# Retention and MLP on one core: merged key and query transfers, W_in rows in head order through split weight transfers, and a rearranged start

## The chip, the core and the metric

The kernel runs on one core of a Trainium2 chip. The metric is device time in microseconds (us); with one core the slowest core is that core. "PE" is TensorE, "PEld" its weight loads, "DVE" VectorE, "ACT" ScalarE, "POOL" GpSimd, "SP" SyncE.

## The reference

Four sequences of 768 tokens with 8 heads of 64 go through a retention layer, and its output through an MLP with weights in float64.

```python
batch, n_heads, seq, head_dim = (4, 8, 768, 64)
n_tokens, d_model, d_ff = (3072, 512, 2048)

for t in range(S):                                     # retention
    state = gamma[None, :, None, None] * state + np.einsum('bhd,bhe->bhde', k[:, :, t], v[:, :, t])
    y[:, :, t] = scale * np.einsum('bhd,bhde->bhe', q[:, :, t], state)
# x = y as (B*S, H*D)
h = x @ w_in                                           # MLP
sp = np.maximum(h, 0.0) + np.log1p(np.exp(-np.abs(h)))
g = h * erf(sp)
return (g @ w_out).astype(np.float32)
```

Only the q, k, v inputs are cast to float32. W_in (512 x 2048) and W_out (2048 x 512) arrive as 8-byte words, and the kernel makes float32 of them on DVE and ACT.

## The kernel before

The tokens are cut into 24 chunks of 128. A chunk's keys, queries and values are 256 KB each, in rows of 64 floats, that is, in packets of 256 bytes. The weights come in 16 pieces of 1 MB, in rows of 256 words, that is, in packets of 2 KB. The chunks fill three rotating buffers; the weight pieces fill four raw areas, each reloaded as soon as its piece is converted.

DVE scales the keys and queries of a chunk, masks its scores, and converts weights between these in a fixed order. Keys and queries are loaded so that heads (0, 3), (1, 2), (4, 7), (5, 6) lie side by side, and that takes four transfers each:

```python
PAIRS = ((0, 3), (1, 2), (4, 7), (5, 6))
MOVES = ((0, 0), (3, 1), (1, 2), (2, 3))
def load(j):
    ...
    for i, src in enumerate((k, q)):
        queue = nc.scalar if i and j < 3 else nc.sync
        for of, to in MOVES:
            queue.dma_start(
                KQ[j][:, i].rearrange("p (a b) d -> p a b d", a=2)[:, :, to],
                src[b, :, now, :].rearrange("(a b) p d -> p a b d", a=2)[:, :, of],
            )
    nc.sync.dma_start(V[j], v[b, :, now, :].rearrange("h p d -> p h d"))

def load_piece(n):                       # a W_in piece: one transfer into all 128 partitions
    ...
    nc.sync.dma_start(
        w.rearrange("p (g f) -> p g f", g=n_k),
        w_in[:, i * 2 * P : (i + 1) * 2 * P].rearrange("(g p) f -> p g f", p=P),
    )
```

The pairing lets the retention output land in PSUM in just the row order that W_in has, so two wide copies per chunk finish it:

```python
def place(h, r):
    return pp[r][h % 2 * D : (h % 2 + 1) * D, h // 4, :]
...
for r in range(2):
    nc.scalar.copy(XC[m][:, r::2, i * C : (i + 1) * C], pp[r][:, :2, :])
```

The start:

```python
nc.scalar.dma_start(d_k, decay_k)
load(0)
for s in range(2):
    nc.scalar.dma_start(d_s[:, s], ...)       # a small transfer, 2 KB each
load(1)
load_piece(0)
load(2)
load_piece(1)
ident = const.tile([P, P], F32, name="ident")
make_identity(nc, ident)
... # 28 dummy transposes on PE
```

Of the kernel before, what the change touches and what calls it, by code (L numbers as in the profile page):

```python
# [12 lines left out]
F32 = mybir.dt.float32  # L13
# [6 lines left out]
P = 128  # L20
# [6 lines left out]



PAIRS = ((0, 3), (1, 2), (4, 7), (5, 6))  # L30
MOVES = ((0, 0), (3, 1), (1, 2), (2, 3))


IN = {"11": 0, "12": 1, "21": 2, "22": 3, "S3": 2, "S1": 4, "S2": 5, "S4": 6}
# [12 lines left out]
def kernel(  # L47
# [13 lines left out]
    nc = tc.nc  # L61
    B, H, S, D = q.shape
# [4 lines left out]
    n_k = d_model // P  # L67
# [4 lines left out]
    DH = d_model // 2  # L72
# [3 lines left out]
    const = ctx.enter_context(tc.tile_pool(name="const", bufs=1))  # L76
# [9 lines left out]
    KQ, V = {}, {}  # L86

    def load(j):
        b, c = divmod(j, NC)
        KQ[j] = loads.tile([P, 2, H, D], F32, name="kq")  # L90
        V[j] = loads.tile([P, H, D], F32, name="v")
        now = slice(c * C, (c + 1) * C)
        for i, src in enumerate((k, q)):

            queue = nc.scalar if i and j < 3 else nc.sync
            for of, to in MOVES:
                queue.dma_start(  # L97
                    KQ[j][:, i].rearrange("p (a b) d -> p a b d", a=2)[:, :, to],
                    src[b, :, now, :].rearrange("(a b) p d -> p a b d", a=2)[:, :, of],
                )  # L100
        nc.sync.dma_start(V[j], v[b, :, now, :].rearrange("h p d -> p h d"))

    kq_s = const.tile([P, NC, 2, H], F32, name="kq_s")
    d_k = const.tile([P, H], F32, name="d_k")
    d_s = const.tile([P, 2, HP], F32, name="d_s")

    w_in_sb = const.tile([P, 2, 7, 2, FG * P], F32, name="w_in_sb")
    w_out_sb = const.tile([P, 2, 7, FG, DH], F32, name="w_out_sb")
# [26 lines left out]
    place = [n % 4 if n < n_p - 4 else (n - n_p + 4) % 3 for n in range(n_p)]  # L135

    def load_piece(n):
        which, i = pieces[n]
        w = raws[place[n]]
        if which == "in":  # L140
            nc.sync.dma_start(
                w.rearrange("p (g f) -> p g f", g=n_k),
                w_in[:, i * 2 * P : (i + 1) * 2 * P].rearrange("(g p) f -> p g f", p=P),
            )
        else:
            for d in range(2):
                nc.sync.dma_start(
                    w.rearrange("p (d f c) -> p d f c", d=2, f=2)[:, d],
                    w_out[i * 2 * P : (i + 1) * 2 * P, d * DH : (d + 1) * DH].rearrange(
                        "(f p) c -> p f c", p=P  # L150
                    ),
                )

    def load_pieces_after(n):
        for later in range(n + 1, n_p):
            if place[later] == place[n]:
                load_piece(later)
                break
# [95 lines left out]
    def pace(n):  # L254

        nonlocal room
        room += n
        while room >= 1:
            next(weight_steps, None)
            room -= 1  # L260

    def need(*what):
        nonlocal room
        while what not in done:
            if next(weight_steps, done) is done:
                next(last_steps)
            room -= 1

    nc.scalar.dma_start(d_k, decay_k)
    load(0)  # L270
    for s in range(2):
        nc.scalar.dma_start(d_s[:, s], decay_s[s * D : s * D + 1, :].to_broadcast([P, HP]))
    load(1)
    load_piece(0)
    load(2)
    load_piece(1)

    ident = const.tile([P, P], F32, name="ident")
    make_identity(nc, ident)

    causal = const.tile([P, C], F32, name="causal")
    nc.gpsimd.memset(causal, 1.0)
# [4 lines left out]
    state = const.tile([P, HP, D], F32, name="state")  # L287
# [4 lines left out]
    def query_scale(c):  # L292
        nc.vector.reciprocal(kq_s[:, c, 1], kq_s[:, c, 0])
        nc.vector.tensor_scalar(kq_s[:, c, 1], kq_s[:, c, 1], unscale, None, op0=ALU.mult)

    def in_pairs(to, of):
        for a, b in MOVES:
            nc.vector.tensor_copy(
                to.rearrange("p (a b) -> p a b", a=2)[:, :, b],
                of.rearrange("p (a b) -> p a b", a=2)[:, :, a],  # L300
            )

    in_pairs(kq_s[:, 0, 0], d_k)
    query_scale(0)

    def other_scales():
        back, by = (const.tile([P, H], F32, name=name) for name in ("back", "by"))
        nc.vector.reciprocal(back, d_s.rearrange("p s h -> p h s"))
        in_pairs(by, back)
        for c in range(1, NC):  # L310
            nc.gpsimd.tensor_tensor(kq_s[:, c, 0], kq_s[:, c - 1, 0], by, op=ALU.mult)
        query_scale(slice(1, NC))


    QT, KT, SC, AM, XC, SU = {}, {}, {}, {}, {}, {}
# [3 lines left out]


    idle = ps_o.tile([P, P], F32, name="o0")
    for _ in range(28):
        nc.tensor.transpose(idle, ident, ident)

    def ret_psum():

        pool = next(psum_turn) if early else ps_r
        return pool.tile([P, HP, C], F32, name="hp" if pool is ps_h else "r")
# [49 lines left out]
    def ret_out(j):  # L378
        c = j % NC
        m, i = divmod(j, JPC)  # L380
        if i == 0:
            XC[m] = ret.tile([P, HP, TCH], F32, name="xT")

        pp = [ret_psum() for _ in range(2)]

        def place(h, r):
            return pp[r][h % 2 * D : (h % 2 + 1) * D, h // 4, :]



        if c:
            for u, pair in enumerate(PAIRS):
                for r, h in enumerate(pair):
                    own = slice(r * D, (r + 1) * D)
                    nc.tensor.matmul(  # L395
                        place(h, r), state[own, u, :], QT[j][own, u, :],
                        start=(h < 4), stop=False, skip_group_check=True,
                    )
        for h in range(H):
            u, r = next((u, pair.index(h)) for u, pair in enumerate(PAIRS) if h in pair)  # L400
            nc.tensor.matmul(  # L401
                place(h, r), V[j][:, h, :], AM[j][:, r, u, :],
                start=(not c and h < 4), stop=True, skip_group_check=True,
            )
        for r in range(2):
            nc.scalar.copy(XC[m][:, r::2, i * C : (i + 1) * C], pp[r][:, :2, :])  # L406
        pace(1.5)

    def ret_state(j):
        c = j % NC  # L410
        if c < NC - 1:
            p = SU[j] = ret_psum()
            for u, pair in enumerate(PAIRS):
                for r, h in enumerate(pair):
                    nc.tensor.matmul(  # L415
                        p[r * D : (r + 1) * D, u, :D], KQ[j][:, 0, 2 * u + r, :], V[j][:, h, :],
                        start=True, stop=True,
                    )
            pace(1)
        if j + 3 < NJ:  # L420
            load(j + 3)
        if j < 2:
            load_piece(j + 2)
# [89 lines left out]
    def chunk_of(g):  # L513
        return TCH // SCH + (g - G0) // 2
# [104 lines left out]
    def put_part(m, step):  # L619
# [26 lines left out]

    K_, T, S_, M, O_, U, A = (
        ret_scale, ret_transpose, ret_scores, ret_mask, ret_out, ret_state, ret_add
    )


    K_(0)
    other_scales()
    T(0)
    n_first = 6
# [40 lines left out]
    j = 2 * JPC  # L696
# [50 lines left out]
    g, m = NG - 1, chunk_of(NG - 1)  # L747
# [47 lines left out]
```

## Time and profile before

| What | Value |
|---|---|
| Time | 754.32 us median of 6 (753.08 to 755.75) |
| Span of the profiled execution | 751.6 us |
| Scaling of chunk 5 | 45.13 us, after a wait of 3.33 us |
| Dense PE stretch begins | 82.93 us |
| 2 KB packets, mean of the whole execution | 93.5 ns |
| 256-byte packets, mean of the whole execution | 18.2 ns |

The groups of transfers of before (what is written <- what is read, engine, count, KB each, median us from issue to landing):

```profile
kq<-in_k_dram SPq DMA_DIRECT2D x96, 64.0 KB, 2.6
...
w_in_sb<-in_moe_w_in_dram SPq DMA_DIRECT2D x6, 1024.0 KB, 5.6
...
w_out_sb<-in_moe_w_in_dram SPq DMA_DIRECT2D x2, 1024.0 KB, 6.8
```

The raw words of W_in land in spare parts of either weight tile, hence two rows for it: 6 + 2 transfers of a whole megabyte, and 96 small ones for the keys. The order of time on SP's queue shows the issues for chunk 5 (start, duration, line, what it fills, count):

```profile
35.34 2.00 SPq L97 DMA_DIRECT2D kq<-in_k_dram  x4
37.39 5.09 SPq L97 DMA_DIRECT2D kq<-in_q_dram  x4
42.52 1.47 SPq L101 DMA_DIRECT2D v<-in_v_dram  x1
```

Nine issues from 35.34 to 43.99 us; the last queries are issued shortly before 42.5 us and the scaling that needs them starts at 45.13.

### The profile page before, as it was taken

The page shows a single profiled execution, that of the slowest core. Times are in us where ns is not written, and L with a number is a line of the kernel's source. Part 1 is how long each engine was busy: PE and PEld are TensorE (multiplying, and loading weights), DVE is VectorE, ACT ScalarE, POOL GpSimd, SP SyncE. Part 2 cuts the span into 40 slices and gives each one's busy share as a digit, 9 for nine tenths or more (in the row PEclk, how much of TensorE's full clock was granted, in tenths as well). Part 3 has the DMA queues.
Part 4 walks back from the last instruction along what each step waited for, and adds up shares of the span by engine and source line. Part 5 has one row for each costly group of instructions (what it writes and reads, how often), then busy time and mean ns, then how long its engine had stood idle before and what let it go on. Part 6 is the DMA issues. An engine that isn't in the chain of part 4 may idle for free.

```text
span 751.6 us, 12027 instructions
## 1 busy us (share of the span) xinstructions
PE 724.5 (96%) x5244; PEld 609.3 (81%) x5244; DVE 353.4 (47%) x470; ACT 274.1 (36%) x319; POOL 32.4 (4%) x28
## 2 busy tenths in 40 slices
PE   6877999999999999999999999999999999999997
PEld 5644444457789999999999999999999999999995
DVE  3878899975554424333243153153163152153323
ACT  1323555341532433424414424424334244324440
POOL 1000200000010110110110110101100000000000
PEclk8999999999999999999999999999999999999999
DMA  8885634101110120120120120110100000000000
GB/s 192 238 227 171 195 117 164 56 0 43 57 43 19 25 71 9 36 72 1 43 72 1 43 71 1 43 51 22 43 29 1 2 29 1 1 29 1 1 29 28
DMA packets 89700, 42.73 MB, mean 57 GB/s; under 512 B 78384, under 2 KB 78384, under 8 KB 89648
## 3 DMA queue, kind: packets, MB, share of 16 engines
q1 hardware_dynamic: 85952, 41.17, 19.7%
q10 hardware_dynamic: 3696, 0.80, 0.5%
q8 instruction: 41, 0.67, 0.4%
q14 instruction: 11, 0.09, 0.0%
HBM read 35.66 MB, written 6.29 MB: 56 GB/s over the span
## 4 chain that ended last, share of the span: by engine, by line
PE 88%; DVE 4%; DMA 4%; ACT 1%; SPq 1%; issue 1%; ACTq 0%; DVEq 0%
PE hp L544 34%; PE o L604 32%; PE o L487 7%; PE hp L474 6%; PE r L361 3%; PE r L401 2%; PE r L348 2%; DMA w_out_sb<-in_moe_w_out_dram 2%; PE r L415 1%; PE r L395 1%; DMA kq<-in_q_dram 1%; DVE am L373 1%; SPq L97 1%; DMA w_in_sb<-in_moe_w_in_dram 1%; DVE kq L339 0%
## 5 line engine op out<-in xcount | busy, mean ns | idle before, releaser
L544 PE MATMUL hp<-xs,w_in_sb 128*128 128x128 f32 x1280 | 158.7, 278 | 0.0
L544 PEld LDWEIGHTS hp<-xs,w_in_sb 128*128 128x128 f32 x1280 | 150.4, 192 | 6.6 <-issue 3.2
L604 PE MATMUL o<-w_out_sb,h 128*128 128x256 f32 x640 | 141.6, 379 | 0.0
L463 DVE TENSOR_TENSOR e<-h,e 128x1024 f32<-128x1024 f32 x44 | 53.6, 1260 | 178.5 <-ACT e L444 178.5
L604 PEld LDWEIGHTS o<-w_out_sb,h 128*128 128x128 f32 x640 | 121.7, 190 | 16.5
L544 PE MATMUL hp<-xT,w_in_sb 128*128 128x128 f32 x960 | 113.7, 275 | 0.0
L544 PEld LDWEIGHTS hp<-xT,w_in_sb 128*128 128x128 f32 x960 | 112.0, 192 | 1.9 <-issue 1.0
L604 PE MATMUL o<-w_out_sb,e 128*128 128x256 f32 x480 | 111.5, 382 | 0.9 <-DVE e L463 0.9
L604 PEld LDWEIGHTS o<-w_out_sb,e 128*128 128x128 f32 x480 | 88.2, 190 | 12.5 <-DVE e L463 1.3
L443 ACT ACT_TABLE_LOAD x24 | 30.8, 1283 | 91.2 <-PE o L604 89.1
L474 PE MATMUL hp<-xT,w_in_sb 128*128 128x512 f32 x128 | 57.6, 605 | 0.0
L572 DVE TENSOR_TENSOR h<-h,hp 128x512 f32<-128x512 f32 x20 | 13.8, 688 | 86.7 <-PE hp L544 86.7
L339 POOL TENSOR_TENSOR kq<-kq,kq_s 128x1024 f32<-128x1024 f32 x15 | 30.3, 2019 | 499.8 <-DMA kq<-in_q_dram 401.1
L474 PEld LDWEIGHTS hp<-xT,w_in_sb 128*128 128x128 f32 x128 | 24.5, 195 | 29.4 <-issue 28.7
L567 DVE TENSOR_TENSOR h<-h,hp 128x512 f32<-128x512 f32 x20 | 13.8, 688 | 71.1 <-ACT h L565 71.1
L443 ACT ACTIVATE e<-h 128x2048 f32<-128x2048 f32 x22 | 42.0, 1910 | 0.2
L444 ACT ACTIVATE e<-e 128x2048 f32<-128x2048 f32 x22 | 42.0, 1910 | 0.2
L406 ACT COPY xT<-r 128x256 f32<-128x256 f32 x42 | 13.9, 375 | 74.8 <-PE r L401 74.8
L570 ACT COPY h<-hp 128x512 f32<-128x512 f32 x20 | 11.7, 585 | 70.8 <-PE hp L544 70.8
L373 DVE TENSOR_TENSOR am<-r,causal 128x512 f32<-128x512 f32 x42 | 27.2, 683 | 20.3 <-PE r L361 15.9
L361 PE MATMUL r<-qT,kT 64*128 64x128 f32 x336 | 29.9, 291 | 4.6 <-ACT qT L354 4.5
L348 PE MATMUL r<-ident,kq 128*128 128x128 f32 x168 | 24.0, 285 | 9.3 <-DMA kq<-in_k_dram 4.9
(91 smaller groups left out, 667.6 us busy)
## 6 DMA issues: line engine op xcount, KB each, us to landing
w_out_sb<-in_moe_w_out_dram SPq DMA_DIRECT2D x14, 512.0 KB, 5.0
kq<-in_k_dram SPq DMA_DIRECT2D x96, 64.0 KB, 2.6
v<-in_v_dram SPq DMA_DIRECT2D x24, 256.0 KB, 3.6
w_in_sb<-in_moe_w_in_dram SPq DMA_DIRECT2D x6, 1024.0 KB, 5.6
out_dram<-r SPq DMA_DIRECT2D x24, 256.0 KB, 2.3
kq<-in_q_dram SPq DMA_DIRECT2D x84, 64.0 KB, 2.5
w_out_sb<-in_moe_w_in_dram SPq DMA_DIRECT2D x2, 1024.0 KB, 6.8
w_in_sb<-in_moe_w_out_dram SPq DMA_DIRECT2D x2, 512.0 KB, 4.9
```

The costliest lines, as they stand in the source:

```text
L339: engine.tensor_tensor(KQ[j], KQ[j], by, op=ALU.mult)
L348: nc.tensor.transpose(p[:, u, :], KQ[j][:, i, 2 * u : 2 * u + 2, :].rearrange("p h d -> p (h d)"), ident,)
L361: nc.tensor.matmul(pp[s][:, hp, :], KT[j][s * D : (s + 1) * D, hp, :], QT[j][s * D : (s + 1) * D, hp, :], start=True, stop=True,)
L373: nc.vector.tensor_tensor(AM[j][:, s], SC[j][s], causal[:, None, :].to_broadcast([P, HP, C]), op=ALU.mult)
L401: nc.tensor.matmul(place(h, r), V[j][:, h, :], AM[j][:, r, u, :], start=(not c and h < 4), stop=True, skip_group_check=True,)
L443: nc.scalar.activation(E[g], HS[g], AF.Softplus)
L444: nc.scalar.activation(E[g], E[g], AF.Erf)
L463: nc.vector.tensor_tensor(E[g][:, half], HS[g][:, half], E[g][:, half], op=ALU.mult)
L474: nc.tensor.matmul(p, w_in_of(ft, kk), XC[0][:, kk, :], start=(kk == 0), stop=(kk == n_k - 1))
L487: nc.tensor.matmul(O[0][tt].rearrange("p (d c) -> p d c", d=2), E[g][:, u * TCH + tt * P : u * TCH + (tt + 1) * P], w_out_of(ft), start=(f ...
L544: nc.tensor.matmul(bank[:, u, :], w_in_sb[:, s, IN[a], kk, u * P : (u + 1) * P], XS[m][b][:, kk, :], start=(p in (1, 2, 5) and u == 0 and ...
L604: nc.tensor.matmul(O[m][i][:, half, :], G[g][a][:, u * P : (u + 1) * P], w_out_sb[:, s, OUT[b], u, :], start=i not in started, stop=(s == ...
```

## The change

The intent: load keys and queries of a chunk in one transfer each, with the heads in their own order, and pay for that in the weights rather than at every chunk. With natural pairs (0, 1), (2, 3) and so on, the retention output comes out in another row order; W_in's rows are loaded in that order, which needs two transfers per piece, each into 64 partitions. Apart from that, the first weight pieces are sent right behind chunk 0, the identity is made first, ten dummy matmuls take the place of 28 transposes, and a tiny ACT copy draws the activation table in early.

```diff
-PAIRS = ((0, 3), (1, 2), (4, 7), (5, 6))
-MOVES = ((0, 0), (3, 1), (1, 2), (2, 3))
+PAIRS = (0, 2, 1, 3)
@@ load
-            for of, to in MOVES:
-                queue.dma_start(... [:, :, to], ... [:, :, of])
+            queue.dma_start(KQ[j][:, i], src[b, :, now, :].rearrange("h p d -> p h d"))
@@ load_piece
-            nc.sync.dma_start(
-                w.rearrange("p (g f) -> p g f", g=n_k),
-                w_in[:, i * 2 * P : (i + 1) * 2 * P].rearrange("(g p) f -> p g f", p=P),
-            )
+            for r in range(2):
+                nc.sync.dma_start(
+                    w[r * D : (r + 1) * D].rearrange("p (g f) -> p g f", g=n_k),
+                    w_in[r * DH : (r + 1) * DH, i * 2 * P : (i + 1) * 2 * P].rearrange(
+                        "(g p) f -> p g f", p=D
+                    ),
+                )
@@ start
+    ident = const.tile([P, P], F32, name="ident")
+    make_identity(nc, ident)
     nc.scalar.dma_start(d_k, decay_k)
     load(0)
+    nc.scalar.copy(idle_out, ident[:, :1])
     for s in range(2):
         nc.scalar.dma_start(d_s[:, s], ...)
+    load_piece(0)
     load(1)
-    load_piece(0)
+    load_piece(1)
     load(2)
-    load_piece(1)
-    ident = const.tile([P, P], F32, name="ident")
-    make_identity(nc, ident)
@@ dummies
-    for _ in range(28):
-        nc.tensor.transpose(idle, ident, ident)
+    for _ in range(10):
+        nc.tensor.matmul(idle, ident, ident, start=True, stop=True)
@@ ret_out
-            return pp[r][h % 2 * D : (h % 2 + 1) * D, h // 4, :]
+            return pp[h % 2][h // 4 * D : (h // 4 + 1) * D, h % 4 // 2, :]
... (the loops over heads follow the natural pairs; a few tiny copies of scales fall away)
```

## The prediction

> **What bounds the kernel now.** I read the engine shares first, then the activity by slices, then ten-microsecond windows, then the chain of waits, and last the order of time on VectorE (DVE) and on the queue of SyncE (SP). From the page:
>
> ```profile
> PE 724.5 (96%) x5244; PEld 609.3 (81%) x5244; DVE 353.4 (47%) x470; ACT 274.1 (36%) x319; POOL 32.4 (4%) x28
> ...
> PE   6877999999999999999999999999999999999997
> ...
> DVE  3878899975554424333243153153163152153323
> ```
>
> Read the slices, not the averages: PE is at 9 from the sixth slice on. Only the first four or five slices (18.8 us each) have room, so a change that leaves the later matmuls alone can only move the moment at which the dense stretch begins. The chain of waits names that moment:
>
> ```profile
> 82.93 13.93 PE hp L474 x32
> 96.86 13.73 PE o L487 x32
> ```
>
> From 82.9 us the chain is PE nearly all the way to 751.6. Before it, the windows (PE, PEld, DVE, ACT, POOL busy; granted clock; DMA share; GB/s):
>
> ```profile
> 0.00:10.00 10.00, 6.12 (x36) 5.64 (x36) 2.67 (x13) 0.00 (x0) 2.15 (x13) 1.00 0.64 137
> 10.00:20.00 10.00, 6.41 (x46) 5.16 (x48) 5.42 (x8) 3.94 (x7) 0.00 (x0) 0.59 1.03 270
> 20.00:30.00 10.00, 8.33 (x124) 6.48 (x120) 7.84 (x11) 3.09 (x6) 0.00 (x0) 0.89 0.64 183
> 30.00:40.00 10.00, 8.64 (x132) 6.87 (x136) 9.64 (x13) 4.61 (x9) 0.00 (x0) 1.00 1.02 308
> 40.00:50.00 10.00, 5.32 (x66) 4.18 (x61) 5.28 (x7) 1.82 (x4) 0.00 (x0) 0.83 0.70 163
> 50.00:60.00 10.00, 9.66 (x65) 5.40 (x64) 9.21 (x11) 4.34 (x7) 0.00 (x0) 1.00 0.89 234
> ```
>
> DVE, which scales keys and queries, masks scores and converts the weights in a fixed order, is nearly full from 22 us on, except at 40:50, where DMA was full just before. The order of time shows what DVE waited for; also why the start is late on ScalarE (ACT):
>
> ```profile
> 10.39 1.28 ACT L354 ACT_TABLE_LOAD   x1 [10.39 <-DMA kq<-in_k_dram]
> ...
> 14.92 0.69 DVE L373 TENSOR_TENSOR am<-r,causal 128x512 f32<-128x512 f32 x1 [4.42 <-PE hp L361]
> ...
> 45.13 1.23 DVE L339 TENSOR_TENSOR kq<-kq,kq_s 128x1024 f32<-128x1024 f32 x1 [3.33 <-DMA kq<-in_q_dram]
> ```
>
> The last line is the key one: the scaling of chunk 5 waits 3.33 us for its keys and queries. What DVE gained earlier ends at that wait. After it DVE waits only for PE (1.28, 0.66, 2.34, 1.04, 1.66 us up to 83 us), in an order that the change does not touch. So the prediction is: when does chunk 5 land?
>
> **What the skill says.** (1) The Trainium skill, "DMA: Bandwidth & Descriptors", section "Rules for kernel authors": merge many small transfers, and two transfers to the two halves of the partitions gain nothing, they serialize. The trace agrees with the first on the issuing side: on SP a 64 KB transfer takes 0.47 us to issue and the 256 KB one for values takes the same 0.47. (2) "SBUF — State Buffer", section "Door 1: The DMA port swizzle": 64 partitions reach only half of the ports; 1 MiB into 64 partitions ran at 196 GB/s, into 128 at 328. The trace of before has no large transfer into 64 partitions, so it shows nothing here; the change makes all of W_in such transfers. (3) "ScalarE: Activation LUTs", section "What ACT_TABLE_LOAD costs": about 1283 ns; here 1.28 us. (4) "TensorE: Matmul & The Clock Gate", section "Part 1: The HAM clock gate": about 3.4 us of work opens the clock, an idle window closes it. Here the clock was 1.00 in the first ten microseconds and 0.50 from 12 to 22, after PE had idled from 8.69 to 12.81.
>
> **The change part by part.** The order of instructions on PE and DVE is the same, apart from the dummies, a few tiny copies, and which head takes which place. The matmul counts and shapes stay (4 row and column patterns as before), so from 83 us on I expect nothing.
>
> *Issue.* Chunk 5 before: SP issues 4 + 4 + 1 transfers from 35.34 to 43.99, 8.65 us, since each also waits until the one eight issues back has landed. After: three issues, 1.4 us, with up to eight whole 256 KB transfers in flight. W_in goes from one transfer to two, +0.47 us per piece, on a queue that then has time. The issue cost is beside other work except where the DMA engines ran dry for it.
>
> *Did they run dry?* In the trace's packet records a 256-byte packet takes 18.2 ns and a 2 KB packet 93.5 ns on one of 16 engines. A chunk is 3 x 1024 small packets: 3072 x 18.2 / 16 = 3.5 us. A weight piece is 512 large ones: 3.0 us. Up to chunk 5 the order needs 6 chunks and 5 pieces (four of W_in, one of W_out): 21.0 + 15.0 = 36 us. Adding up the DMA share in two-microsecond windows to 44.8 us gives 37.2 us (instruction fetch is in it). First data flows at about 2.2 us, so 42.6 us held 37.2 us of work: 5.4 us were dry (0.45 at 8:10, 0.36 to 0.65 at 22:28, 0.48 at 42:44). With deep queues I give back all but 1 us: 2.2 + 37.2 + 1.0 + 0.3 to the scaling = 40.7, against 45.13. Gain 4.4 us.
>
> *Can DVE use it?* Before, from the first mask (14.92) to the end of the masks of chunk 4 (41.8) are 26.9 us, of which 0.88 + 1.31 + 0.29 = 2.5 are waits: 24.4 of work. The first mask moves up by 1.1 (keys and queries of chunk 0 land at about 5.2 instead of 6.31, two issues instead of eight), 3.4 (the copy after the transposes could begin at 8.24 and began at 11.68, behind ACT's issues and the table load, both out of the way now), and 0.95 (scores took 2.1 us at half clock, 1.15 at 33 us at full): to about 9.5. Then 9.5 + 24.4 = 33.9, plus some 2.5 of waits for chunks 1 and 2, which now stand behind weights: 36.4. That is before 40.7, so DMA and not DVE sets chunk 5, and 4.3 us of these early gains are lost in that wait.
>
> *Dummies, table, tiny copies.* Ten f32 matmuls instead of 28 transposes (5.02 us from 1.43) end before the first real transpose at about 6.5; they, the early table load, the saved 0.3 + 0.3 us of copies all act before chunk 5's wait. Beyond it they are worth nothing, except a clock that may stay open in chunk 5's step (at most the 1.28 + 0.66 of waits there; I count 0).
>
> *W_in in halves.* Working from the skill's ratio, an estimate: 3.0 x 328 / 196 = 5.0 us per piece, 2.0 more, 8.0 for the four in front of chunk 5. Queries of chunks 1 and 2, on ACT's ring, may fill part of it; I take off 2: 6 us. That would eat the 4.4 and 1.6 more.
>
> Sum without the port effect: 754.3 - 4.4 = 749.9. With it: 754.3 + 1.6 = 755.9.
>
> **Rivals.** *A, ports bound the halves* (755.9, between 754 and 757.5). For: the page's measurement, and DMA at 1.02 of its share from 30 to 40 us, so any lengthening there reaches chunk 5 directly. Against: no transfer of this trace shows it, and small packets of another ring run in between. *B, DMA only gets denser* (749.9, between 747.5 and 751.5). For: the dry windows. Against: chunk loads still wait for a free buffer of three. *C, DVE becomes the bound after the shift*: DVE runs full from 50.6 to 147 us. For: the second projection starts at 124.17 with its last weights ready at 119.78, only 4.4 us of room. Against: all of DVE after chunk 5 moves with it, so room stays; only if PE moved alone by more than 4.4 us would it cost. Worth at most 1 us. *D, nothing moves*: the chunk-5 wait is replaced at chunk 6 or 7. Against: chunk 6 needs 3.5 us more of DMA and its scaling comes 6.66 us later (51.79 - 45.13). It would leave 754.3.
>
> **Range and chances.** I weigh B 6 and A 4 in 10: 0.6 x 749.9 + 0.4 x 755.9 = 752.3; I say 752.0. The range takes both: 747 to 757. Two per cent are 15 us; all DVE waits between 14.92 and 83 us are 12.8 us, so faster by 2% has a chance of 0.01; slower by 2% would need the halves to lengthen by twice what I fear or a wait in the dense part: 0.01. Within 2%: 0.98.
>
> **What would show it.** The table load before 4 us; first mask near 9.5 us; the scaling of chunk 5 at 40 to 41 us (B) or 46 to 47 (A); the dense stretch starting 37.8 us after it, as now (82.93 - 45.13); all later distances unchanged. Ports: 2 KB packets of W_in lasting far over 93 ns while those of W_out do not. The prediction is wrong if the dense stretch itself becomes longer, if chunk 5 no longer ends DVE's longest wait, or if DVE rather than DMA holds it.

## The result, and the profile after

The changed kernel is correct and took 758.90 us in the median (757.76 to 759.55, 6 runs) against 754.32 (753.08 to 755.75, 6 runs). The ratio is 1.0059, with a 95% interval of 1.0045 to 1.0072. It is slower by a little over half a per cent, which counts as the same within 2%, but it lies outside the predicted range of 747 to 757. All ratios here are the mean time of one kernel's runs over the mean of the other's runs of the same rounds, so they differ a little from the ratio of the medians quoted.

From the page of the kernel after, engine shares and two rows of slices:

```profile
PE 726.7 (96%) x5236; PEld 611.5 (81%) x5236; DVE 353.3 (47%) x463; ACT 274.8 (36%) x320; POOL 31.9 (4%) x28
...
PE   6857999999999999999999999999999999999997
...
DVE  3759899985463243243153053163163152153323
```

The engines do the same work, and PE is dense from the fifth slice on, as before; the third slice has fallen from 7 to 5. The chain of waits between 40 and 105 us (start, duration, what) shows why:

```profile
38.05 10.89 DMA kq<-in_q_dram
...
49.03 1.24 DVE kq L331
...
87.26 13.93 PE hp L466 x32
```

The queries of chunk 5 were issued from 38.05 us and are the link of the chain until the scaling starts at 49.03; before, it started at 45.13. The dense stretch begins at 87.26 instead of 82.93 us: 4.33 of the 4.7 us by which the profiled spans differ (756.3 - 751.6). The remaining 0.36 us arises near 180 us, where PE waits 0.74 us for a mask instead of 0.38.

The order of time in the kernel after, on ACT and then on DVE (start, duration, what; in brackets, how long the engine had been idle before it and what ended that):

```profile
1.74 1.28 ACT L273 ACT_TABLE_LOAD   x1 [1.74 <-PEq L770]
```

```profile
9.56 0.20 DVE L301 RECIPROCAL by<-d_s 128x8 f32<-128x8 f32 x1 [2.34 <-DMA d_s<-decay_s_dram]
11.76 0.68 DVE L365 TENSOR_TENSOR am<-r,causal 128x512 f32<-128x512 f32 x1
...
15.06 1.23 DVE L331 TENSOR_TENSOR kq<-kq,kq_s 128x1024 f32<-128x1024 f32 x1 [2.03 <-DMA kq<-in_q_dram]
...
49.03 1.23 DVE L331 TENSOR_TENSOR kq<-kq,kq_s 128x1024 f32<-128x1024 f32 x1 [6.18 <-DMA kq<-in_q_dram]
```

The early part came in as intended: the table load is at 1.74 us and the first mask at 11.76 instead of 14.92. Then chunk 1 waits 2.03 us, and chunk 5 waits 6.18 us where it waited 3.33. DVE reached chunk 5 ready, and the transfers were not.

The ten-microsecond windows after (columns as in the prediction's):

```profile
0.00:10.00 10.00, 6.30 (x36) 5.87 (x38) 1.98 (x5) 2.55 (x4) 1.29 (x9) 0.93 0.83 176
10.00:20.00 10.00, 6.93 (x58) 5.52 (x58) 5.95 (x9) 2.96 (x5) 0.87 (x5) 0.50 1.22 207
20.00:30.00 10.00, 8.18 (x98) 6.65 (x100) 6.59 (x8) 1.82 (x4) 0.00 (x0) 0.71 1.03 199
30.00:40.00 10.00, 8.38 (x132) 6.26 (x124) 9.64 (x12) 4.62 (x9) 0.00 (x0) 1.00 1.18 214
40.00:50.00 10.00, 2.81 (x48) 1.96 (x46) 3.82 (x6) 0.65 (x2) 0.00 (x0) 0.81 0.95 227
```

Read the last two columns. The dry windows are gone: the DMA share is at or above 0.95 from 10 to 50 us. But what it moves is 199 to 227 GB/s, where the full windows of before moved 270 and 308. The engines are busier without moving more. (A share above 1 means that packet records overlap in time, so the share is no exact measure of capacity. The rate also depends on the mix of packets: from the means of the kernel before I estimate 16 x 256 B / 18.2 ns = 225 GB/s for small packets alone and 16 x 2048 B / 93.5 ns = 350 for large ones.)

So it is best to compare stretches that hold almost only large packets. The kernel after has two of them close together, one with halves of W_in, the other with the piece of W_out behind them, which comes over all 128 partitions:

```profile
38.00:40.00 2.00, 1.83 (x28) 1.53 (x29) 1.97 (x2) 1.14 (x3) 0.00 (x0) 1.00 1.07 214
...
42.00:44.00 2.00, 1.32 (x16) 0.83 (x16) 0.85 (x2) 0.39 (x2) 0.00 (x0) 1.00 1.04 357
```

At nearly the same share, the halves move 214 GB/s and the full-width piece 357.

The groups of transfers after point the same way:

```profile
kq<-in_k_dram SPq DMA_DIRECT2D x24, 256.0 KB, 3.3
...
w_in_sb<-in_moe_w_in_dram SPq DMA_DIRECT2D x12, 512.0 KB, 6.8
...
w_out_sb<-in_moe_w_in_dram SPq DMA_DIRECT2D x4, 512.0 KB, 10.1
```

Half a megabyte of W_in takes longer to land (6.8 and 10.1 us) than the whole megabyte did (5.6 and 6.8), though this includes what a half waits behind the other. The packet records say the same at a finer grain. I took the packets that start before chunk 5 is scaled; each kernel has 2560 large ones there, four pieces of W_in and one of W_out:

| Kernel | Mean of 256 B, ns | Mean (median) of 2 KB, ns | Sum of all packets / 16, us | Chunk 5 scaled at, us |
|---|---|---|---|---|
| before | 19.0 | 93.2 (84) | 36.9 | 45.13 |
| after | 23.9 | 142.4 (149) | 51.1 | 49.03 |
| after, W_in full width (first experiment) | 20.5 | 96.4 (84) | 39.8 | 41.92 |
| after, W_in in two full-width transfers (second) | 21.0 | 97.1 (84) | 40.9 | 41.13 |
| before, W_in in halves (third) | 20.8 | 142.2 (151) | 47.1 | 51.68 |

The prediction had named this sign of the ports: in the kernel after, the first 2048 of these large packets, nearly all of them of W_in, have a median of 156 ns, and the last 512, of W_out, one of 89.

### The profile page after: what moved, and what is told of

It reads as the page before. It is cut to its first block, busy times and chain, and to the rows that moved or that the text cites. A ratio compares the mean times of both kernels' runs of the same rounds, so it can differ in the third digit from the quotient of the medians.

```text
span 756.3 us, 11745 instructions
## 1 busy us (share of the span) xinstructions
PE 726.7 (96%) x5236; PEld 611.5 (81%) x5236; DVE 353.3 (47%) x463; ACT 274.8 (36%) x320; POOL 31.9 (4%) x28
## 4 chain that ended last, share of the span: by engine, by line
PE 89%; DMA 4%; DVE 3%; ACT 1%; SPq 1%; issue 1%; DVEq 0%; ACTq 0%
PE hp L536 33%; PE o L596 31%; PE o L479 7%; PE hp L466 6%; DMA kq<-in_q_dram 3%; PE r L340 2%; PE r L393 2%; PE r L353 2%; PE r L407 2%; PE r L388 1%; DMA w_in_sb<-in_moe_w_in_dram 1%; PE hp L353 1%; DVE am L365 1%; DVE kq L331 0%; DMA kq<-in_k_dram 0%
## 5 line engine op out<-in xcount | busy, mean ns | idle before, releaser
L455 DVE TENSOR_TENSOR e<-h,e 128x1024 f32<-128x1024 f32 x44 | 51.9, 1222 | 180.1 <-ACT e L436 180.1
L340 PEld LDWEIGHTS r<-ident,kq 128*128 128x128 f32 x168 | 20.6, 151 | 16.0 <-issue 9.4
## 6 DMA issues: line engine op xcount, KB each, us to landing
w_out_sb<-in_moe_w_in_dram SPq DMA_DIRECT2D x4, 512.0 KB, 10.1
```

What stands on the lines that cost most here:

```text
L340: nc.tensor.transpose(p[:, u, :], KQ[j][:, i, 2 * u : 2 * u + 2, :].rearrange("p h d -> p (h d)"), ident,)
L455: nc.vector.tensor_tensor(E[g][:, half], HS[g][:, half], E[g][:, half], op=ALU.mult)
```

## The experiments

My theory was that the 64-partition halves of W_in cost more than the merged loads gain, through the time that each packet takes. The rivals were that the number of transfers is at fault, that the new start is, or that the gain of merging was never there. Twelve runs were made (the last is the kernel of the fourth once more), each timed with five rounds beside the kernel before, on three chips. The medians of before were 755.02, 755.11 and 754.71 us, so I compare across the calls only through ratios or distances to before.

### W_in in one full-width transfer again

```diff
-            for r in range(2):
-                nc.sync.dma_start(w[r * D : (r + 1) * D]..., w_in[r * DH : (r + 1) * DH, ...]...)
+            nc.sync.dma_start(
+                w.rearrange("p (g f) -> p g f", g=n_k),
+                w_in[:, i * 2 * P : (i + 1) * 2 * P].rearrange("(g p) f -> p g f", p=P),
+            )
```

The rows of W_in are then in the wrong order for this kernel, so the result is wrong (relative error 1.206). The amount and kind of work stay.

> The changed kernel with one thing put back: every W_in piece comes in one transfer over all 128 partitions in the rows' old order, so the result is wrong on purpose (weights of other heads), while every instruction on PE, DVE and ACT is the same. Ports theory[...]: the 2 KB packets of W_in fall from about 160 ns to about 84 to 93 ns, small packets beside them from 28 to 18 ns, chunk 5 is scaled at 40 to 42 us instead of 49.0, and the time is 749 to 752 us. Rival one (crowding: weights ahead of chunk 1 and deeper queues delay chunk 5): 758 to 759, chunk 5 still at 48 to 49. Rival two (something in the dense part): only the first 90 us stay the same and 758 remains.

It took 750.06 us (747.31 to 750.62), ratio 0.9933 (0.9913 to 0.9953). The order of time on DVE:

```profile
41.92 1.22 DVE L328 TENSOR_TENSOR kq<-kq,kq_s 128x1024 f32<-128x1024 f32 x1 [1.63 <-DMA kq<-in_q_dram]
```

Two of its windows:

```profile
10.00:20.00 10.00, 6.74 (x58) 5.41 (x60) 5.64 (x10) 2.11 (x5) 1.01 (x5) 0.53 1.08 239
...
30.00:40.00 10.00, 8.22 (x132) 6.38 (x130) 9.64 (x13) 3.98 (x7) 0.00 (x0) 1.00 1.02 290
```

With the transfers full width, chunk 5 is scaled 7.1 us earlier than after the change, its wait is 1.63 us, and the engines move 290 GB/s at a share of 1.02 where they moved 214 at 1.18. Against before, the mean is 5.1 us lower (749.74 to 754.82); the changed kernel's was 4.4 us higher (758.71 to 754.29). The halves thus cost 9.5 us.

### Two transfers per piece, but each into 128 partitions

```diff
-                    w[r * D : (r + 1) * D].rearrange("p (g f) -> p g f", g=n_k),
+                    w.rearrange("p (g f) -> p g f", g=n_k)[:, 2 * r : 2 * r + 2],
...
-                        "(g p) f -> p g f", p=D
+                        "(g p) f -> p g f", p=P
```

This keeps the count and the size of the transfers (512 KB) and changes only the width. Its output is wrong, which doesn't matter for the time.

> The changed kernel with every W_in piece in two transfers, as it has them, but each over all 128 partitions and half of the columns of the tile (two of the four row groups); result wrong on purpose. It has the count of transfers of the change without the half partitions. Ports theory: within 1 us of the run with one full transfer, 749 to 752. Rival (the second transfer itself, its issue and its place in the eight waits, costs): 755 to 759.

It took 749.13 us (747.62 to 750.17), ratio 0.9923 (0.9905 to 0.9942), with chunk 5 at 41.13 us and 2 KB packets nearly as fast as before (97.1 ns in the mean to 93.2). The number of transfers costs nothing that these runs can show; the width does.

### The kernel before with W_in in halves

```diff
-            nc.sync.dma_start(w.rearrange(...), w_in[...].rearrange("(g p) f -> p g f", p=P))
+            for r in range(2):
+                nc.sync.dma_start(
+                    w[r * D : (r + 1) * D].rearrange("p (g f) -> p g f", g=n_k),
+                    w_in[...].rearrange("(g p) f -> p g f", p=P)[r * D : (r + 1) * D],
+                )
```

This adds the suspected cost alone and is correct.

> The kernel before with one thing added: every W_in piece comes in two transfers of 64 partitions each, same rows to the same places, right result. Ports theory: four pieces in front of chunk 5 get 2.0 to 2.5 us longer each; the dry time of 5.4 us before chunk 5 hides a part, so chunk 5 is scaled at 49 to 53 us instead of 45.1 and the time is 758 to 762. Rivals (order, depth of queues): no change, 754 to 755.

It took 760.95 us (760.37 to 762.15), ratio 1.0082 (1.0063 to 1.0102). The order of time on DVE:

```profile
51.68 1.22 DVE L342 TENSOR_TENSOR kq<-kq,kq_s 128x1024 f32<-128x1024 f32 x1 [5.05 <-DMA kq<-in_q_dram]
```

Chunk 5 comes 6.6 us later than in the kernel before, and the time rises by 6.3 us in the mean (761.15 to 754.82). The cost is shown from both sides: taken out of the kernel after, and put into the kernel before. It is smaller there, which fits the dry windows of before that take up part of it; that explanation I only argue.

### Full-width W_in, and the rows put right in the copies

```diff
         for r in range(2):
-            nc.scalar.copy(XC[m][:, r::2, i * C : (i + 1) * C], pp[r][:, :2, :])
+            for s in range(2):
+                nc.scalar.copy(
+                    XC[m][r * D : (r + 1) * D, 2 * s : 2 * s + 2, i * C : (i + 1) * C],
+                    pp[r][s * D : (s + 1) * D, :2, :],
+                )
```

This is the first experiment with its error mended: four copies of 64 partitions per chunk move the rows on their way out of PSUM.

> A version with a right result and full-width W_in: the changed kernel, W_in in one transfer over 128 partitions in the old order, and the outputs of the retention put in that order by four ACT copies of 64 partitions per chunk instead of two of 128. Ports theory: the gain of the run with one full transfer, less what two more copies of about 0.37 us cost where PE waits for them in the first 90 us (up to 0.75 us per chunk on the path for chunks 6 and 7): 749.5 to 754. Rivals: 758 or more.

It is correct and took 751.37 us (749.88 to 752.88), ratio 0.9954 (0.9934 to 0.9974): faster than both kernels. Against the first experiment in the same rounds the copies cost 1.6 us in the mean (751.35 to 749.74), where the runs of either kernel spread over some 3 us. Here are the ACT groups of a sibling of this kernel (g1, below) for those copies, and its scaling of chunk 5 follows with that run:

```profile
L395 ACT COPY xT<-r 64x256 f32<-64x256 f32 x84 | 30.8, 367 | 73.5 <-PE r L389 72.5
```

A copy of 64 partitions takes 367 ns where one of 128 takes 376 (in the kernel after), so halving the partitions saves next to nothing and the count doubles.

### The kernel after with the old start

The next four kernels (f1 to f4) shared their rounds. The first has the whole start of before put back: weights behind chunks 1 and 2, identity after the loads, 28 transposes, no early table load.

```diff
-    load_piece(0)
     load(1)
-    load_piece(1)
+    load_piece(0)
     load(2)
+    load_piece(1)
... (identity after the loads, 28 transposes, no tiny ACT copy)
```

> The changed kernel with its whole start put back: weights behind chunks 1 and 2, identity made after the loads, 28 dummy transposes, no table load ahead. Single transfers for keys and queries and halves of W_in stay. Theory (what comes before the wait of chunk 5 is worth nothing; bytes in front of it are the same): 758 to 760, chunk 5 scaled at 48.5 to 50. Rival (weights ahead of chunk 1 are what delays it): 755 to 756.5. Rival (the new start gains time): 761 or more.

It took 759.79 us (758.55 to 760.77), ratio 1.0066 (1.0050 to 1.0082). The interval overlaps that of the change as a whole (1.0045 to 1.0072). Its first mask is at 10.18 us, earlier than 11.76, yet chunk 5 waits 7.14 us, until 50.24. With halves, no effect of the start can be told from the scatter: what DVE gains is lost in the wait for chunk 5.

### Full-width W_in with the old start

The same edit of the start, on the first experiment. What is left of the change is the merged transfers for keys and queries, with what follows from them. Its output is wrong, which doesn't matter for the time.

> The changed kernel with full-width W_in (result wrong on purpose, as in the first run) and the whole start put back: of the change only the single transfers of keys and queries are left. Theory: the single transfers carry all of the gain of about 5 us, so 749 to 751, chunk 5 scaled at 41 to 43 us. Rival (the new start carries it): 753 to 755.

It took 747.79 us (747.60 to 749.69), ratio 0.9915 (0.9900 to 0.9930), the lowest of all, a little better than I had expected. Chunk 5 is scaled at 39.56 us, after 2.89 us of waiting. Merging the transfers is worth 6.5 us in the mean (754.72 to 748.19).

### The kernel before with the new start alone

```diff
+    ident = const.tile([P, P], F32, name="ident")
+    make_identity(nc, ident)
     nc.scalar.dma_start(d_k, decay_k)
     load(0)
+    nc.scalar.copy(idle_out, ident[:, :1])
     ...
+    load_piece(0)
     load(1)
+    load_piece(1)
     load(2)
... (ten matmuls for 28 transposes)
```

> The kernel before with only the new start: weights behind chunk 0, identity first, table load ahead, ten dummy matmuls; four transfers each for keys and queries, full-width W_in, right result. Theory: within 1 us of before (754 to 756), because chunk 5 waits for the same bytes and the same 8.65 us of issues. Rival: 751 or less.

It took 758.79 us (757.21 to 759.17), ratio 1.0052 (1.0037 to 1.0067). I had expected it to be neutral, and it costs 3.8 us in the mean (758.53 to 754.72), with chunk 5 scaled at 49.94 us instead of 45.13. The order of time on ACT with its queue, and then on DVE, shows where:

```profile
11.54 4.34 ACTq L97 DMA_DIRECT2D kq<-in_q_dram  x8
15.92 0.59 ACT L357 COPY kT<-r 128x512 f32<-128x512 f32 x1 [10.96 <-DMA kq<-in_q_dram]
```

```profile
12.76 0.20 DVE L311 RECIPROCAL back<-d_s 128x8 f32<-128x8 f32 x1 [4.87 <-DMA d_s<-decay_s_dram]
...
19.16 0.69 DVE L376 TENSOR_TENSOR am<-r,causal 128x512 f32<-128x512 f32 x1 [3.70 <-PE hp L364]
```

ACT issues the eight query transfers of chunks 1 and 2 from 11.54 to 15.88 us. They wait behind the weights: the first of them goes out just after the first megabyte of W_in, the transfer eight issues back on both queues together, has landed (at 11.52 us, by the trace's landing records). ACT's first real copy, which comes after these issues in its order, begins at 15.92 us, and the first mask at 19.16 instead of 14.92. Buffers come free late, and the transfers after them start late:

```profile
20.00:30.00 10.00, 9.36 (x112) 7.30 (x112) 8.62 (x11) 4.47 (x9) 0.00 (x0) 1.00 0.33 75
```

The share of 0.33 at 75 GB/s in this window is DMA run dry. The small decay transfer is issued at 6.61 us instead of 3.77, in the same queue, and lands by 12.76 us instead of 7.82.

### The two halves from two engines

```diff
-                nc.sync.dma_start(
+                (nc.scalar if r and n < 4 else nc.sync).dma_start(
```

In the kernel after, the second halves of the first four W_in pieces go out from ACT, so that transfers into both halves are in flight together (in the trace, for one, from 30.51 us, when one is issued on ACT, to 37.00, when the other from SP lands).

> The changed kernel with the second half of the first four W_in pieces issued from ACT instead of SP, so that packets of both halves can be on the way at once; right result. If the halves only suffer because one ring brings them one after the other, 2 KB packets of the first four pieces fall toward 90 to 120 ns and the time to 750 to 755. If two halves side by side gain little[...], 757 to 760. ACT may be held up by its issues; then its copies come later and the time is above 759.

It took 759.35 us (758.68 to 760.81), ratio 1.0065 (1.0050 to 1.0080), no better than the kernel after. Two windows:

```profile
10.00:20.00 10.00, 3.73 (x30) 3.14 (x32) 2.08 (x5) 1.07 (x2) 1.02 (x5) 0.50 1.20 204
...
30.00:40.00 10.00, 8.06 (x130) 6.03 (x130) 9.49 (x13) 3.96 (x7) 0.00 (x0) 1.00 1.11 205
```

The rate stays at 205 GB/s at a full share. The run is not clean: ACT is held up by its own issues, and the first mask falls back to 17.60 us. What it tells is the rate, not the time.

### The four copies with the parts of the start

Four kernels: the four-copies kernel with the whole old start (g1), with the old load order but the new identity, table load and dummies (g2), with the new load order but the old rest (g3), and unchanged (g4). All are correct.

```diff
# g1: weights behind chunks 1 and 2; identity after the loads; 28 transposes; no early table load
# g2: as g4, but:
-    load_piece(0)
     load(1)
-    load_piece(1)
+    load_piece(0)
     load(2)
+    load_piece(1)
# g3: as g1, but weights right behind chunk 0
```

> The correct kernel with full-width W_in and four copies per chunk, with the whole start of the kernel before (weights behind chunks 1 and 2, identity after the loads, 28 transposes, no early table load). Theory (the new start costs, because the small decay transfer and the queries of chunks 1 and 2 queue behind 2 MB of weights): 748 to 749.5 us, about 2 us under the same kernel with the new start in the same rounds, first mask at 10.5 to 11.5 us, scaling of chunk 5 at 40 to 41.5 us. Rival (the 2 us between the two batches were chip to chip and the start is neutral here): within 0.7 us of that kernel, 750.5 to 752.

> The four-copies kernel with the old order of loads, but identity first, table load ahead, ten dummy matmuls. If the order of the weights is what costs: 748 to 749.5 us, like the whole old start, first mask 10.5 to 12. If the identity and the ACT copy ahead of the decay loads are what costs (they delay the decay transfers and the first queries by some 1 to 2 us): 750 to 751.5, first mask at 13 or later.

> The four-copies kernel with the new order of loads (weights right behind chunk 0), but the old identity, 28 transposes and no early table load. If the order costs: 750.5 to 752 us, first mask 13.5 to 15. If it does not: 748 to 749.5.

> The four-copies kernel with the new start once more, for the same rounds: 750.5 to 752 us, scaling of chunk 5 at 42 to 43.5 us, dense stretch from about 81.4 us, whatever the theory; only the distance of the other three from it is the question.

| Kernel | Median, us | Ratio to before (95%) | First mask, us | Chunk 5, us | Dense stretch, us |
|---|---|---|---|---|---|
| g1, whole old start | 750.54 | 0.9941 (0.9927 to 0.9955) | 10.25 | 39.57 | 78.91 |
| g2, old order, new rest | 750.63 | 0.9945 (0.9933 to 0.9958) | 12.82 | 40.52 | 80.76 |
| g3, new order, old rest | 750.05 | 0.9934 (0.9921 to 0.9948) | 11.82 | 40.41 | 79.18 |
| g4, new start | 751.27 | 0.9952 (0.9939 to 0.9964) | 13.40 | 41.62 | 80.34 |

The scaling of chunk 5 in g1:

```profile
39.57 1.23 DVE L327 TENSOR_TENSOR kq<-kq,kq_s 128x1024 f32<-128x1024 f32 x1 [1.89 <-DMA kq<-in_q_dram]
```

I had expected the old start to gain 2 us and one of its two parts to carry it. The profiles do show chunk 5 at 39.57 us with the old start and 41.62 with the new, but the times differ by only 0.9 us in the mean (750.28 and 751.20) and the intervals of their ratios overlap. Neither part alone explains even that: g3 is as fast as g1. So the theory of 2 us missed, and so, narrowly, did the rival's 0.7. With merged transfers and full-width W_in the new start gains nothing and costs about a microsecond (by their distances to before, the first experiment and f2 give 1.4); which part of it does so stays open.

All four beat both kernels; g1 and g3 are some 0.6% below before.

## Why the prediction was wrong, step by step

**The view of the bound: right.** The first 83 us were the place, and the scaling of chunk 5 the hinge. The dense stretch began 38.2 us after it (37.8 before), and nothing after it moved by more than 0.4 us.

**The gain of merging: right in mechanism and nearly in size.** Without the halves, the prediction's sum gave chunk 5 at 40.7 us and a time of 749.9. The first experiment measured 41.92 and 750.06 us, and the old start 39.56 and 747.79. The dry windows did fill: from 20 to 30 and from 40 to 50 us the DMA share was 0.90 and 1.04 in the first experiment, against 0.64 and 0.70 before. That its time agrees to 0.2 us is partly luck: against before, chunk 5 came 3.2 us earlier and the mean time fell by 5.1, where both had been put at 4.4.

**The issue term: wrong, without effect on the sum.** "After: three issues, 1.4 us" for chunk 5 came to 9.3 us: 0.41, 4.29 and 4.58 us in the order of time on SP's queue. I had taken the price of an issue from moments when the queue was short. These long ones fell where the DMA share was about 1, so I read them as issues that wait for room. It is the same with full-width W_in (8.2 us in the first experiment). Of the three, the keys and queries, for which the scaling waits, took 4.8 us against 7.1 before, so some issue time was saved, but far less than I had put; what else the merging gained is that the engines no longer ran dry.

**The halves: the term was mis-sized, by what I took off it.** The estimate from the skill's ratio was 2.0 us more per piece, 8.0 for four. The large packets bear it out: 2560 x (142.4 - 93.2) ns / 16 = 7.9 us. Then came the step that failed: "Queries of chunks 1 and 2, on ACT's ring, may fill part of it; I take off 2: 6 us." The traces do not bear out that allowance. The small packets that ran beside the halves became slower as well: a mean of 23.9 ns, against 20.5 in the first experiment, where W_in is full width, which is 18408 x 3.4 ns / 16 = 3.9 us more of packet time. (Before, the mean was 19.0; the rise from there to 20.5 came without any halves and is not theirs.) Removing the halves brought chunk 5 forward by 7.1 us (49.03 to 41.92) and the time by 9.5, where I had put 6; against the 8.0, at most 0.9 of the 2 us taken off was there. The second is larger than the first for reasons of counting, mostly. The profiled spans differ by 7.6 us (756.3 and 748.7); the means of all runs differ by 9.0, for the profile of the kernel after was one of its shorter executions (the six have spans of 756.0 to 757.8) and that of the first experiment one of its longer (745.6 to 748.9); and the last 0.5 us is the difference of before (754.29 and 754.82).

**The weighing: wrong.** I gave B, "DMA only gets denser", six chances in ten, although the term that separates A from B was a measurement of the skill against nothing but the hope of overlap. The gain of B came in full (the first experiment), and A's loss on top of it: 758.9, 3 us above A's point of 755.9 and 1.4 above A's upper end of 757.5. A mixture of two alternatives put the point where neither was, and my upper limit of 757 lay below that end.

**The start: wrong in the details, near right in the sum.** The first mask came at 11.76 us, not 9.5. It was held by the decay transfer, which landed by 9.56 us instead of 7.82 because it shares the queues with the weights (g1 and g3 differ in the order of loads alone, and there it landed by 7.44 and 9.63 us); I had counted only keys, copy and clock. The clock did not stay open either: 0.50 from 10 to 20 us. That the early gains are worth nothing beyond chunk 5's wait was right for this kernel (758.90 us with the new start, 759.79 with the old). It is not true in general, since the same start cost the kernel before 3.8 us.

**The rivals C and D** did not come about. D would have left chunk 5's gain to be eaten by chunk 6; with full-width W_in, the gain arrived at the end.

**Slips of reading, without effect on the outcome.** PE is at 9 from the fifth slice on, not the sixth. The DMA share from 8 to 10 us was 0.55; 0.45 is what was missing. Added up packet by packet, the DMA work up to 44.8 us is 36.7 us, not 37.2. And DVE, said to run full from 50.6 us, waited 2.34, 1.04 and 1.66 us before 83, as the prediction itself lists.

Put together from mean times, adding the parts one after the other to the kernel before and the new start last: merged transfers -6.5 us, halves +11.6 (759.82 - 748.19), new start -0.7 (the change as a whole is 4.4 above before, the kernel with the old start 5.1). The sum is +4.4 us. The last of the three is inside the scatter. The sizes depend on what else is there: the halves cost 11.6 us with merged transfers and the old start, 9.5 with the new start, and 6.3 in the kernel before; the new start alone cost that kernel 3.8.

## What to carry to other kernels

A layout that is got "for free" by letting transfers write 64 partitions at a time was paid for here, and by other transfers in flight too: look at GB/s beside the busy share, since a full share at a lower rate, for a like mix of packets, was the sign (214 against 357 GB/s). When a term separates two rivals and is backed by a measurement, do not discount it for overlap unless the trace shows idle capacity there. And watch for a small transfer that the first step needs, or an engine's issues ahead of its first real work, queued behind megabytes of weights: the new start did this to the kernel before and cost it 3.8 us.

## What the Trainium skill lacked or had wrong

- "SBUF — State Buffer", section "Door 1: The DMA port swizzle": its ratio for 1 MiB, 196 to 328 GB/s (1.67), held: the kernel after moved 214 GB/s with halves of W_in and 357 with the full-width W_out behind them (1.67). In time per packet the ratio was larger: the median of 2 KB packets from 15 to 20 us was 156 ns after and 84 ns before (1.86). The page does not say that full-width packets of other transfers slow down beside halves: the mean of the 256-byte packets before chunk 5 was 23.9 ns with halves and 20.5 without (after and the first experiment), 20.8 and 19.0 in the kernel before with and without them.
- The same page, section "Can I just issue two DMAs to hit both halves?", states a gain of only 6% for two at once. The run with halves from two engines shows no gain at all: 204 and 205 GB/s at a full share, where the kernel after had 207 and 214 in the same windows.
- "DMA: Bandwidth & Descriptors", section "Rules for kernel authors", gives shared engines as the reason why two halves do not pay. Two transfers on the same engines that are each full width cost nothing here (749.13 us against 750.06 for one), so the width is what costs. That it does so through the ports, as the SBUF page has it, fits, but no run placed 64 partitions otherwise than as 0 to 63 and 64 to 127, which could have told the ports from the width itself.
- The same page, section "Issuing engines are not separate DMA queues", calls the sequencer's time to start a transfer usually small. When transfers are queued, it was not: up to 4.58 us for one 256 KB transfer on SP in the kernel after, where eight transfers on ACT in the kernel before with the new start took 4.34 us together. No page that I read gives a number for an issue into full queues.
